# Half of each w_in piece on a second DMA queue, and a new written order for every engine, in an attention block followed by a feed-forward layer

## The chip, the cores and the metric

The kernel runs on one core of one Trainium2 chip. The metric is the device time of one execution in microseconds (us), lower is better. Three runs of the kernel before took 711.14, 709.20 and 710.52 us; the median is 710.52.

## What is computed

Inputs are x (8 batches, 8 heads, 512 tokens, 64 wide), state (8, 8, 32, 64), w_in (512 x 2048) and w_out (2048 x 512), all float32.

```python
scores = x @ state.T / sqrt(D);  a  = softmax(scores);   xread = a  @ state
scores2 = state @ x.T / sqrt(D); a2 = softmax(scores2);  sread = a2 @ x
t = concat([xread, sread], axis=2)      # 544 rows a head; heads side by side: 4352 x 512
h = t @ w_in
out = (h * erf(softplus(h))) @ w_out
```

## The kernel before, in words

The batches are worked off one after another. Batch 0 goes its own way at the start (`begin0`, `mixed0`, `first0`, `serf0`, `second0`); the others use seven products in place of eight for each pair of block matrices, in the first product (`first_product`, L930) and in the second (`second_product`, L1014, and a twice nested form, `twice_product`, L1250). `mixed` and `mixed0` multiply the states of a batch by w_in; the attention weights (tile aT) times that (tile m) give h.

d_ff is cut into 16 columns of 128. A **piece** of w_in is one such column: 512 x 128, laid in SBUF as 128 partitions of 4 runs of 128 floats. `rows_in` (L524) loads a piece in two DMAs, partitions 0 to 63 (e = 0) and 64 to 127 (e = 1). Pieces 0 to 7 are fetched at the start, in four pairs, by `fetch_in` through SyncE's queue; pieces 8 to 15 ("late") through GpSimd's queue between batches, next to the late pieces of w_out (`fetch_out`). The early part of w_out comes in four pairs of 1 MB on SyncE's queue (L564).

A piece lands in one of three staging tiles, raw 0 to 2, and is converted (`convert`): two ScalarE passes (L547 writes the piece, L549 works on raw in place), then three VectorE passes (L551, L553, L555). After the last of these its raw tile is free for the next fetch. The early pairs go in this order with their tiles: w_in 0-1 (raw 0), w_in 2-3 (raw 1), w_out 0-1 (raw 2), w_out 2-3 (raw 0), w_in 4-5 (raw 1), w_in 6-7 (raw 2), w_out 4-5 (raw 0), w_out 6-7 (raw 1).

The start of batch 0: x arrives in four DMAs, TensorE transposes it (L404), the copies x0 to x3 bring it to SBUF, scores (L430), copies s00 to s11, transposes of the scores (L436), softmax on VectorE and ScalarE (L455, L457, L460, L462, L465), transposes of a (L440), the copies ta0 and ta1 into aT, and the first products of batch 0 (L602) with the m tiles of `mixed0` (L585). softplus (L609), erf (L614) and a multiplication (L618) follow, then the second products (L627). `warm` (L114) issues filler products.

What sets the order: every step is recorded by `op` with an engine, a cost and the regions that it reads and writes. ORDER (L163) is a table written out by hand: for each engine, the sequence in which its recorded steps are issued. `emit` lays the steps of all engines into one program by a small simulation with the costs, and `in_order` ties each engine to its sequence. An engine issues strictly in that order, so a step that waits holds all steps behind it on its engine, DMA issues included. `either` puts a copy out of PSUM on VectorE if its name is in BY_VECTOR (L153), else on ScalarE.

Of the kernel before, what the change touches and what calls it, by code (L numbers as in the profile page):

```python
# [17 lines left out]
def kernel(  # L18
# [17 lines left out]
    nc = tc.nc  # L36
# [6 lines left out]
    NK = d_model // P  # L43
# [55 lines left out]
    begun = traced()  # L99
# [39 lines left out]
    def op(engine, cost, at, go, reads=(), writes=(), table=None, land=0.0, pipe=0.0):  # L139
# [14 lines left out]
        x0 x1 x2 s10 ta1 m021 u1""".split())  # L154

    def either(name, cost, out, in_, at, reads, writes):
# [3 lines left out]
        else:  # L160
# [4 lines left out]
            8 0-1 5 2 15 3 6 4 9 7 12 16 13 10 17 11 14 18-21 23 22 25 24 37 45 61 36 60 53 44 52 62  # L165
            26 46 55 27 38 29 28 47 30-32 49 48 41 39 68 34 51 33 50 35 43 66-67 40 65 42 69 63 84
            54 70 58-59 72-73 64 74 71 75 77 76 80 57 85 81 78 86 56 79 87 83 82 89 88 93-94 90 122
            121 97-98 124 123 91 125 128 95-96 127 99 126 101 92 102-103 131 104 129-130 132 100 109
            105-106 110 133 107-108 134-135 111 113 112 114 136 138 115-116 168 140-142 169-171
            117-119 175 144 143 120 145 172 146 137 173 148-149 147 177-178 150 174 179 156 152-153  # L170
            151 157 176 180 154 139 181 155 182-183 160 185 158 161-163 215-216 159 218 217 187-189
            219 190 164-167 195 220 196 221-222 184 191 225 224 223 199 226 192 200 227 201-202 197
            186 228 193-194 198 229-230 207 232 208-210 203 262 204-205 265 206 264 266 263 211 234
            212 267 235 213-214 236 269 231 238 237 239-240 272 250 268 241-242 271 273 246 243 247
            233 248 270 244 249 275 274 245 251-252 254 276 255 253 256-257 277 281 279 282 278 309
            283 285 310 312 286 284 313 311 258 287 259-260 316 261 293 314-315 289 318-319 288 294
            280 320 290-291 321 317 292 295 322 296-297 323-324 301 355 302 298 303-304 356 299-300
            325 358 305-306 359 307 357 326 308 327 361 360 334 329 362 336 328 335 365 337 364 338
            331 363 366 330 332 367 340 339 368 348 333 397 341 398 342 399 401 343 350 349 344 352
            402 351 345 353 346-347 354 369 400 376 370 378 377 379-380 371 381-382 372-373 390 374  # L180
            403-404 375 405 383 406 384-387 407-410 391 425 392 426 393-394 431 388 432 389 429-430
            427 395 428 433-434 396 415 435-437 439 416 411 438 413 412 440 417 414 419 456 455 420
            418 458 423 457 459 421-422 462 460 424 461 465 443 445 464 466 463 446 467-468 441-442
            444 447 449 470 450 469 448 451 453 499 454 452 502 500-501 471 503 506 478 504 472-473
            479 474 480 505 482 509 481 475 483 508 476 510 477 507 511 485 512 484 486 492 488 514
            487 513 493-494 489 543 490 496 495 545 497 546 544 491 547 498 550 548 522 515 524 549
            526 517 516 519 553 523 552 554 525 551 555 527 518 520 528 556 536 557-558 521 537-538
            529 539-540 587 531 530 533 532 542 590 541 566 589 588 535 568 594 591 567 534 570
            592-593 569 559 597 560-561 598 595 563 596 562 599 572 564 600 571 565 602 601 580 573
            632 631 575 582 581 574 577 634 633 576 583-584 635 578 585-586 636 638 610 579 637  # L190
            640-641 612 603 642 611 613-614 639 615 643 604 616 605-606 644 607 645 608 646 609 624
            617 625-626 619 627 675 618 621 620 678 628 622 677 630 629 654 679 655 657 623 656 676
            682 647 658 680-681 648-650 659 685 684 660 651 686 683 668 687 652 688 653 689 661 690
            670 662-664 669 671 719-720 672 665 673 721 674 722 666 726 667 723 691 698 724 700 725
            693 692 694 729 702 699 701 730 703 727 695 728 732 731 696 704 733 712 734 714 697 713
            705 763 715-716 707 706 766 764 709 708 717 765 710 718 711 742 767 743 745 744 735
            768-769 737 736 746 738 770 747 739 773 772 748 774 771 740 775-776 756 741 757 749
            758-759 751 750 752-753 760 754-755 761-762 777 784 778-780 786 781 785 788 787 789 783
            790 782 791 798 793 792 795 794 800 796-797 799 802 805 801 807 806 803 809 808 804
            810-811""",  # L200
        ACT: """
            0-1 3 10-11 5 4 2 13 12 6-7 16-17 30 9 31 15 33 14 8 32 19 59 18 58 34 36 35 38 40 20-21
            39 37 41 22-24 43 42 25-27 44 46-47 45 48-50 53 52 51 61 29 60 64 56 54 67 55 62 57 68
            63 70 97 69 28 98 109 71 108 73 101 72 74 66 105 75 80 102 99 82 100 76-77 83 103 79 78
            89 104 84 81 90 139-140 137-138 85 141 88 86 142 87 152 65 93 154 153 94 155 106-107
            95-96 91 148 92 156 110 161 143 149 163 144-146 164 162 157 111 158 160 112 165 168 113
            150 166-167 175 174 159 147 114 169-170 177-178 176 171 117 115 179 189 151 190 116 119
            118 172-173 191 185 180 192 182 193 198 181 120 183 200 195 199 123 201 203 194 124 186
            121 202 122 204 184 205 187 211-212 197 214 213 196 125 215 206-207 216 226 208 188 209
            227-228 130 127 129 126 210 128 229 222 219 230 235-237 135 217 238 220 218 232-233 239  # L210
            134 224 240 231 131 221 133 136 223 241 248-249 132 243 234 250-251 242 252-253 263 244
            265 225 245 266 246 256 264 247 257 254 267 272 255 274 259 273 275 271 278 269 258 277
            268 261 270 276 280 279 281 285-286 260 282 262 288 287 289 283 290 300 284 302 301 291
            296 303 292 304 309 311 310 293-294 312 314 313 295 315 307 297 316 308 305 298 323 322
            306 325 324 317-321 347 299 349-350 326 348 327 351 332 356 334 333 328 358 357 355 335
            353 330 359 329 352 354 331 360 362 336 363 361 364-365 337 366 342 389 367 343 368 338
            345 344 339-340 346 341 390 369 374-375 377 376 370-372 391 373 379 378 392 380 393 384
            396 395 382 394 397 381 385 402 398-399 386-387 404 400-401 403 383 405-406 409 388 416
            410 417-418 415 408 407 420 411-413 422 421 414 423 425 424 429 426 431 428 432 430 435
            433 436 434 427 437-441 419 442-445 466 468 467 446 469 451 472 470 452 475 448 454 447  # L220
            453 477 449 476 478 474 480 471 450 455 479 456 473 481-485 491 461 457 488 486 458
            489-490 459 462 487 512 464 513 460 514 465 463 515 497-498 492-493 516 521 500 523 518
            495 524 499 494 527 522 525 528 501 496 507 519 526 517 534 520 529-530 508 502 536 531
            535 537 510 503 509 532-533 558 505 560 504 559 511 543 561 544 506 562 567 538 546 569
            564 539 570 541 545 571 568 566 540 574 573 542 563 565 583 582 580 575 547 572 548 553
            576-577 581 549 604 578 606 551 554 556 550 607 555 605 557 579 552 589 608 613 615 610
            590 614 591 616 592 584 612 585 619 586 617 587 621 611 626 593 588 620 628 618 609 599
            629 594 622-623 595 600-601 624 627 650 625 597 602 652 596 603 635 653 598 651 636-637
            630 638 656 654 659 661 631 657 633 662 639 655 645 658 663 632 665 660 666 664 634 672
            667 640 668-669 674-675 646 670 673 641 671 648 647 696 642-643 697-698 644 699 676 649  # L230
            681-682 700 705 707 684 677 708 703 683 704 679 678 706 702 701 709 711 685 712 718 713
            691 680 720 719 710 721 714 686 692 715-716 742 717 694 687 689 693 688 695 744 727 690
            743 745 722 748 728 730 750 723 746 724 751 729 725 753 749 731 747 752 754 726 756-757
            755 758 737 759-760 732 761-762 733 763 738 734-735 740 736 739 764 741 769 765 770
            766-767 772 771 773 768 774 779 775 777 776 780 778 784 781-783""",
# [1469 lines left out]
```

## Time and profile before

| | |
|---|---|
| median of three runs | 710.52 us |
| the profiled execution | 708.29 us |
| its span, first to last instruction | 706.5 us |
| TensorE busy | 693.0 us (98%) |
| VectorE busy | 592.3 us (84%) |
| ScalarE busy | 469.6 us (66%) |
| GpSimd busy | 89.8 us (13%) |
| mean granted TensorE clock | 0.997 |
| SyncE's and ScalarE's DMA queues | 61.88 and 0.52 MB |
| GpSimd's DMA queue | 29.63 MB |

How to read it: PE is TensorE, PEld its weight loads, DVE VectorE, ACT ScalarE, POOL GpSimd, SP SyncE; a q behind a name is the engine's sequencer, which issues DMAs. L627 is line 627 of the kernel. A row of the timeline has the start, the duration, the engine, the line, the operation, out<-in, shapes and count, and in brackets the idle time before it with what ended it. A row of the windows has a stretch, its length, busy time and count of instructions for PE, PEld, DVE, ACT and POOL, the granted clock (1.00 is full), the busy share of the 16 DMA engines and GB/s. The line "DMA to landing" gives the least, median and largest time from issue to landing. One float32 product is two MATMUL records.

### The profile page before, as it was taken

Reading aid. Unit: us, or ns where it says so; the run is one execution under the profiler, and the core shown is the slowest. Engines: PE = TensorE matmul, PEld = TensorE weight load, DVE = VectorE, ACT = ScalarE, POOL = GpSimd, SP = SyncE. Lnnn points to the kernel's source line nnn. Section 1 sums busy time; section 2 is a strip of 40 time slices with the busy share of each in tenths; the row PEclk is TensorE's granted clock in tenths of the full one; section 3 lists DMA queues with packets and bytes.
Section 4 is the critical chain, followed back from the end, with each engine's and each line's share of the span. In section 5 each row is a group of like instructions: output and inputs, shape, how many; then the busy total and the mean of one; then the engine's idle time right before and its main releaser. Section 6 shows DMA issues by size and latency. Waiting matters only on the chain.

```text
span 706.5 us, 13126 instructions
## 1 busy us (share of the span) xinstructions
PE 693.0 (98%) x5163; PEld 579.7 (82%) x5163; DVE 592.3 (84%) x986; ACT 469.6 (66%) x852; POOL 89.8 (13%) x101
## 2 busy tenths in 40 slices
PE   8899999999999999999999999999999999999997
PEld 7334568787878878799999879898989898989996
DVE  5889999999999989797945489696869695877897
ACT  5887798878688474837254674838585757575741
POOL 0001101103010100000100100121023214052222
PEclk9999999999999999999999999999999999999999
DMA  9876998777796926221365410325156535285645
GB/s 238 196 192 120 257 235 208 191 179 210 177 291 140 313 97 187 91 83 31 109 169 221 116 53 30 83 32 97 16 97 75 98 45 98 46 105 61 100 65 104
DMA packets 132620, 92.85 MB, mean 131 GB/s; under 512 B 92624, under 2 KB 119632, under 8 KB 132048
## 3 DMA queue, kind: packets, MB, share of 16 engines
q1 hardware_dynamic: 113088, 61.88, 32.7%
q0 software_dynamic: 18928, 29.63, 23.6%
q8 instruction: 40, 0.66, 0.4%
q10 hardware_dynamic: 544, 0.52, 0.2%
q14 instruction: 20, 0.16, 0.1%
HBM read 50.86 MB, written 41.16 MB: 130 GB/s over the span
## 4 chain that ended last, share of the span: by engine, by line
PE 84%; DVE 6%; DMA 2%; ACT 2%; issue 1%; DVEq 0%; SPq 0%
PE o L1250 28%; PE h L930 18%; PE o L1014 17%; PE at L930 7%; PE o L1433 4%; PE h L1384 3%; DMA raw<-in_moe_w_out_dram 2%; PE h L831 2%; PE at L831 2%; PE at L794 1%; PE at L1384 1%; PE h L689 1%; DVE w_in L1232 1%; DVE ring L981 1%; DVE ring L970 1%
## 5 line engine op out<-in xcount | busy, mean ns | idle before, releaser
L942 ACT COPY ring<-h 128x512 f32<-128x512 f32 x120 | 69.1, 587 | 72.9 <-PE h L930 67.5
L930 PE MATMUL h<-aT,m 128*128 128x256 f32 x360 | 91.4, 381 | 0.2 <-ACT ring L942 0.2
L970 DVE TENSOR_TENSOR ring<-ring 128x1024 f32<-128x1024 f32 (+1 forms) x64 | 72.9, 1151 | 22.3 <-ACT ring L967 22.3
L1014 PE MATMUL o<-w_out,ring 128*128 128x256 f32 x320 | 78.0, 382 | 0.0
L952 ACT ACTIVATE ring<-ring 128x512 f32<-128x512 f32 x120 | 72.6, 635 | 3.9 <-DVE ring L944 3.3
L930 PEld LDWEIGHTS h<-aT,m 128*128 128x128 f32 x360 | 65.3, 190 | 10.5 <-ACT ring L942 1.3
L981 DVE TENSOR_TENSOR ring<-ring 128x1024 f32<-128x1024 f32 x60 | 72.5, 1217 | 0.3
L1014 PEld LDWEIGHTS o<-w_out,ring 128*128 128x128 f32 x320 | 59.7, 190 | 15.6 <-issue 5.2
L1250 PE MATMUL o<-w_out,w_in 128*128 128x128 f32 x512 | 69.6, 276 | 0.0
L1250 PEld LDWEIGHTS o<-w_out,w_in 128*128 128x128 f32 x512 | 64.7, 192 | 3.6 <-issue 0.8
L1250 PE MATMUL o<-w_out,ring 128*128 128x128 f32 x480 | 64.8, 276 | 0.0
L1250 PEld LDWEIGHTS o<-w_out,ring 128*128 128x128 f32 x480 | 60.4, 192 | 3.7 <-DVE ot L1265 0.8
L967 ACT ACTIVATE ring<-ring 128x1024 f32<-128x1024 f32 (+1 forms) x64 | 62.7, 1004 | 0.2
L1014 PE MATMUL o<-raw,ring 128*128 128x256 f32 x240 | 59.2, 381 | 0.0
L1014 PEld LDWEIGHTS o<-raw,ring 128*128 128x128 f32 x240 | 45.2, 190 | 7.9 <-issue 1.7
L1250 PE MATMUL o<-raw,ring 128*128 128x128 f32 x360 | 49.7, 275 | 0.0
L1250 PEld LDWEIGHTS o<-raw,ring 128*128 128x128 f32 x360 | 46.0, 192 | 1.9 <-DVE oo L1265 0.8
L1170 POOL DMA_DIRECT2D out_dram<-oo x16 | 23.4, 1462 | 174.6 <-ACT o L1281 104.0
L1250 PE MATMUL o<-raw,xT 128*128 128x128 f32 x320 | 41.1, 276 | 0.2 <-DVE m L1265 0.2
L1250 PEld LDWEIGHTS o<-raw,xT 128*128 128x128 f32 x320 | 38.7, 192 | 1.6 <-issue 0.8
L1281 ACT COPY o<-o 128x256 f32<-128x256 f32 (+1 forms) x41 | 13.5, 330 | 26.8 <-PE o L1250 17.8
L930 PE MATMUL h<-sy,m 128*128 128x256 f32 x120 | 31.1, 382 | 0.0
(269 smaller groups left out, 1421.5 us busy)
## 6 DMA issues: line engine op xcount, KB each, us to landing
x<-in_x_dram SPq DMA_DIRECT2D x30, 256.0 KB, 4.6
xq<-in_x_dram SPq DMA_DIRECT2D x24, 256.0 KB, 4.8
out_dram<-oo SPq DMA_DIRECT2D x10, 512.0 KB, 3.7
raw<-in_moe_w_in_dram SPq DMA_DIRECT2D x16, 256.0 KB, 5.2
raw<-in_moe_w_out_dram SPq DMA_DIRECT2D x4, 1024.0 KB, 7.9
raw<-in_moe_w_in_dram POOLq DMA_DIRECT2D x16, 256.0 KB, 5.3
raw<-in_moe_w_out_dram POOLq DMA_DIRECT2D x8, 512.0 KB, 4.3
kept_a<-aT SPq DMA_DIRECT2D x8, 512.0 KB, 4.7
```

Source lines behind the costliest of these rows:

```text
L831: nc.tensor.matmul(out=bank(names[e])[q, :], lhsT=st[r, b, q], rhs=of_group[2 * u + j][r, :, i, :], start=True, stop=True)
L930: nc.tensor.matmul(out=out_[:, i], lhsT=x_[:, q:q + P], rhs=y_, start=(start and i == 0), stop=(i == 1), skip_group_check=not start)
L942: op(ACT, 0.5, t, lambda: nc.scalar.copy(out_(), view(bank(name))), [name], w)
L952: op(ACT, 0.53, t, lambda: nc.scalar.activation(out=part(splane, k), in_=part(hplane, k), func=ACTF.Softplus), area(hplane, ks=[k], os=[o] ...
L967: op(ACT, 0.085 + 0.875 * share, at + n, lambda s_=s_: nc.scalar.activation(out=s_, in_=s_, func=ACTF.Erf), [], area(splane, ks=[k], os=os ...
L970: op(DVE, 0.065 + 1.075 * share, at + n + 1, lambda s_=s_, h_=h_: tt(s_, s_, h_, op=ALU.mult), area(hplane, ks=[k], os=os), area(splane, k ...
L981: op(DVE, 1.14, at + k, lambda k=k, x_=x_, y_=y_, how=how: tt(get("h", k), get(*x_), get(*y_), op=how), area(v[x_[0]], ks=[x_[1]]) + area( ...
L1014: nc.tensor.matmul(out=view(name)[:, h], lhsT=lhs[:, i, :], rhs=weight_of[n]()[:, u, i, :], start=(start and h == 0 and i == 0), stop=(h = ...
L1170: op(GP, 1.2, t, lambda: nc.gpsimd.dma_start(out=quad(r, c), in_=one(v), accum_op=ALU.add), every(*v), [("out", b, r, c)], land=3.0, pipe=2.0)
L1250: nc.tensor.matmul(out=out_[:, Q2 * k:Q2 * k + Q2], lhsT=lhs[:, k, i], rhs=rhs[:, i], start=first, stop=(k == len(ns) - 1 and i == 1), ski ...
L1384: nc.tensor.matmul(out=bank(bk)[:, P * i:P * i + P], lhsT=x_[:, i, k], rhs=y_[:, k], start=(start and i == 0 and k == 0), stop=(i == GF - ...
L1433: nc.tensor.matmul(out=bank("o%d" % bk)[:, E2 * c:E2 * c + E2], lhsT=ring[:, w_[w], plane, k][:, i, :], rhs=weight_of[n]()[:, u, i, :], st ...
```

## The change

`rows_in` takes two queues, one for each half of the partitions. The first half of an early piece stays on SyncE's queue. The second half goes through ScalarE's queue for pieces 0 and 1 and through GpSimd's for pieces 2 to 7. Late pieces have both halves on GpSimd's queue, as before.

```diff
-    def rows_in(on, to, f, n):
-        for e in range(2):
+    def rows_in(queues, to, f, n):
+        for e, on in enumerate(queues):
             on.dma_start(out=to[D * e:D * e + D],
                          in_=moe_w_in[NI * D * e:NI * D * (e + 1), P * f:P * (f + n)].rearrange(
                              "(k d) f -> d k f", d=D).bitcast(U32))

     def fetch_in(f, k, h, at, late=False):
-        how, on = late_load if late else ((SP, 0.9), nc.sync)
-        op(*how, at, lambda: rows_in(on, half(k, h).rearrange("p (a b) -> p a b", a=NK), f, 1),
-           [("out0", 1)] * late, RAW(k, [h]), land=3.0 * late, pipe=1.7)
-
-    late_load = (GP, 2.0), nc.gpsimd
+        queues = (nc.gpsimd if late else nc.sync, nc.scalar if f < 2 else nc.gpsimd)
+        op(GP if late else SP, 2.0 if late else 0.5, at, lambda: rows_in(
+            queues, half(k, h).rearrange("p (a b) -> p a b", a=NK), f, 1),
+           [("out0", 1)] * late, RAW(k, [h]), land=(3.0 if f > 1 else 0.0),
+           pipe=2.5 if late else 1.7)
```

Which copies VectorE makes is chosen anew, and ORDER is a new table for all five engines (not shown in full: it is a list of step numbers). The simulation in `emit` now always takes the engine whose next step can begin first, where it ran each engine as far as it could.

```diff
     BY_VECTOR = set("""
-        x0 x1 x2 s10 ta1 m021 u1""".split())
+        x0 x1 s01 ta0 m010 m011 m020 u0 u1""".split())
```

What the new order does to the built program, in the lines of the kernel before:

- TensorE: 2611 matrix instructions before and after. The start has 8 + 5 + 3 + 14 filler products where it had 2 + 8 + 3 + 17. Of the first L602 products the second pair now comes first, with transposes of the states and one `mixed0` among the others.
- VectorE after the last L465: m copy, aT copy (ta0), m copy, then the conversions; before: a scale, w_out, w_in (both conversions), then the aT copy (ta1).
- ScalarE: two DMA issues at the head (the second halves of pieces 0 and 1). The m copies of `mixed0(1, 0)` stand ahead of the conversion of w_out 4-5 instead of behind it, and the conversion of w_out 6-7 behind softplus and erf of the next two first products instead of ahead of them. 838 instructions instead of 840: two table loads fewer.
- SyncE: the second half of batch 1's xq loads (four DMAs of 128 KB, L93) stands ahead of the load of w_out 6-7 instead of behind it.
- GpSimd: six half pieces at the head of its queue.
- From batch 1 on, the steps of all engines are in another sequence; the last 158 matrix instructions stand together at the end in both.

More of the change, by code (lines that the diff above doesn't have):

```diff
@@ L170 @@
[L170 to L184, printed above, removed]
@@ new lines @@
+            0-2 5 3 6 8 15 9 13 4 7 16 12 10 17 11 14 20 23 18 21 19 22 25 24 44 36-37 60 53 52 61
+            45 26 38 27 29 28 47 30-32 46 63 48 64 49 39 56 50 34 51 54 43 33 41-42 68 55 40 35 70
+            69 84 59 66-67 73 72 74 71 62 65 75 77 76 80 58 78 81 85 57 79 82 86 83 93 88 87 94
+            89-90 97 121 98 122 124 123 125 95 128 126 96 99 127 101 91 131 102 129 103 132 130 92
+            100 133 105-106 134 107 104 135 109-110 108 136 113-115 111 116 138 112 168 140-142 170
+            143 117 171 118 148 119 169 175 149 172 120 137 173 144 174 145 177 156 178 150 157 179
@@ new lines @@
+            176 152 180 146 181-182 151 147 158 139 153 159 183 154-155 185 160-161 216 187 162-163
+            215 188-190 217 164 218 165 184 219 191 166 192 220 222 167 193 195 221 199 225 196 224
+            186 226 223 200 227 201 194 229 228 197 202 198 230 232 207-209 203 262 210 204 265
+            205-206 263 266 231 264 211-212 234-235 213 236-237 269 267 242-243 214 271 244 268
+            246-248 272 233 238-240 249-250 273 270 245 274 241 275-276 254-255 277 251-252 279 253
+            256-257 309 281-283 310 258 311 284 259-260 312 316 289 278 261 290 313 285 291 314 286
@@ L301, in emit @@
         while any(queue.values()):
-            before = len(end)
+            ready = []
             for e, line in queue.items():
-                while line and all(m in end for m in ops[line[0]][4]):
-                    n = line.popleft()
-                    _, cost, _, _, needs, table, land, pipe = ops[n]
-                    begin[n] = max([free[e]] + [end[m] + LAG[ops[m][0]] * (
-                        ops[m][0] != e or ops[m][7] > 0) for m in needs])
-                    if table not in (None, loaded):
-                        cost, loaded = cost + 1.28, table
-                    end[n] = free[e] = begin[n] + cost
-                    if pipe:
-                        piped = max(piped, begin[n]) + pipe
-                        end[n] = max(piped, free[e]) + (land or FIXED)
-                        if e == SP:
-                            free[e] = max(free[e], piped - AHEAD)
-            assert len(end) > before
+                if line and all(m in end for m in ops[line[0]][4]):
+                    n = line[0]
+                    ready.append((max([free[e]] + [end[m] + LAG[ops[m][0]] * (
+                        ops[m][0] != e or ops[m][7] > 0) for m in ops[n][4]]), n, e))
+            begun, n, e = min(ready)
+            queue[e].popleft()
+            begin[n] = begun
+            _, cost, _, _, _, table, land, pipe = ops[n]
+            if table not in (None, loaded):
+                cost, loaded = cost + 1.28, table
+            end[n] = free[e] = begun + cost
+            if pipe:
+                piped = max(piped, begun) + pipe
+                end[n] = max(piped, free[e]) + (land or FIXED)
+                if e == SP:
+                    free[e] = max(free[e], piped - AHEAD)
         order = sorted(begin, key=lambda n: (begin[n], n))
```

205 lines of the change are left out of this document (105 added, 100 removed), and 6 rows, old and new, of the table ORDER.

## The prediction

> **What bounds the kernel now.** First the page's heading, then busy time by stage, then the stretches with gaps.
>
> ```profile
> span 706.5 us, 13126 instructions
> ```
> ```profile
> 70.00:200.00 130.00, 129.77 (x936) 99.47 (x935) 128.37 (x226) 105.48 (x185) 18.64 (x32) 1.00 0.86 212
> 200.00:660.00 460.00, 459.74 (x3452) 407.50 (x3451) 367.70 (x603) 292.03 (x549) 57.73 (x51) 1.00 0.45 103
> ```
> Columns: length, busy PE, PEld, DVE, ACT, POOL, granted clock, DMA share, GB/s. From 70 to 660 us TensorE lacks 0.23 + 0.26 = 0.5 us. The change touches no product, and both builds issue 2611 matmuls, so nothing is to be won there. VectorE misses only 1.6 us of the 130 up to 200, so there is something to lose.
>
> ```profile
> 5.00:10.00 5.00, 5.00 (x67) 4.15 (x66) 2.36 (x4) 1.90 (x4) 0.00 (x0) 1.00 1.12 239
> 10.00:15.00 5.00, 3.20 (x64) 2.19 (x63) 4.74 (x10) 3.40 (x8) 0.00 (x0) 1.00 1.08 307
> 15.00:20.00 5.00, 4.35 (x50) 3.74 (x49) 4.86 (x11) 2.64 (x5) 0.00 (x0) 1.00 1.08 258
> 20.00:25.00 5.00, 2.13 (x6) 1.25 (x7) 3.80 (x8) 4.50 (x8) 0.00 (x0) 0.82 1.04 227
> ...
> 40.00:45.00 5.00, 4.20 (x24) 1.16 (x22) 3.89 (x6) 3.75 (x5) 0.00 (x0) 1.00 1.07 362
> 45.00:50.00 5.00, 4.80 (x26) 1.96 (x27) 3.98 (x6) 3.77 (x5) 0.00 (x0) 1.00 0.48 77
> 50.00:55.00 5.00, 4.53 (x12) 1.77 (x10) 4.63 (x6) 4.94 (x8) 0.00 (x0) 1.00 0.00 0
> 55.00:60.00 5.00, 4.83 (x24) 1.66 (x23) 4.97 (x7) 4.73 (x7) 0.00 (x0) 1.00 0.36 59
> ```
> ```profile
> 700.00:706.50 6.50, 1.98 (x18) 1.79 (x17) 2.34 (x9) 0.00 (x0) 0.00 (x0) 0.95 0.39 124
> ```
> Before 25 us the DMA engines are full and VectorE is nearly so, while TensorE partly runs filler products. From 40 to 60 its pauses sum to 0.80 + 0.20 + 0.47 + 0.17 = 1.6 us. The last 4.5 us are the drain, which ends in the same 158 products in both builds. So the end is set by when the first large product (L602) starts, plus a fixed queue of products, plus pauses. That start, in order of time:
>
> ```profile
> 20.36 0.69 DVE L465 TENSOR_TENSOR ring<-ring,z1b 128x512 f32<-128x512 f32 x1
> 20.50 1.17 ACT L549 ACTIVATE raw<-raw 128x1024 uint32<-128x1024 uint32 x1 [2.86 <-DMA raw<-in_moe_w_in_dram]
> ...
> 21.11 0.66 PE L440 MATMUL o<-ident,ring 128*128 128x128 f32 x4 [1.76 <-DVE ring L465]
> ...
> 21.71 1.11 ACT L547 ACTIVATE w_in<-raw 128x1024 f32<-128x1024 f32 x1
> 22.73 0.58 ACT L161 COPY aT<-o 128x512 f32<-128x512 f32 x1
> ...
> 23.19 0.28 ACT L161 COPY m<-h 128x128 f32<-128x128 f32 x1
> ...
> 23.47 0.68 DVE L159 COPY aT<-o 128x512 f32<-128x512 f32 x1
> 23.52 5.21 PE L602 MATMUL h<-aT,m 128*128 128x512 f32 x8 [1.76 <-ACT m L161]
> ```
> ScalarE stands 2.86 us before the conversion of w_in pieces 2 and 3, whose DMA lands at 20.5; the copies of aT and m that L602 needs are queued behind it and end at 23.5.
>
> **The change part by part.** *Issues.*
>
> ```profile
> 0.00:5.00 5.00, 3.64 (x17) 3.64 (x18) 0.00 (x0) 1.28 (x1) 0.69 (x6) 1.00 0.63 177
> ```
> ```profile
> 1.74 1.41 SPq L526 DMA_DIRECT2D raw<-in_moe_w_in_dram  x2
> ...
> 3.83 1.41 SPq L526 DMA_DIRECT2D raw<-in_moe_w_in_dram  x2
> 5.29 0.60 SPq L564 DMA_DIRECT2D raw<-in_moe_w_out_dram  x1
> 6.11 2.85 SPq L526 DMA_DIRECT2D raw<-in_moe_w_in_dram  x4
> ```
> A half piece costs SyncE about 0.7 us. Four of the first eight leave it (2.8 us), so its last early issue ends near 9.0 - 2.8 = 6.2. ScalarE takes two (1.4 us), in a stretch where it has one instruction of 1.28 us to do. GpSimd, idle then, issues the second halves of pieces 2 and 3 from about 1.4 us on. Earlier issue is not earlier landing: the DMA share is above 1 from 5 us, so the same bytes fill the engines until about 20. What can be won is the beginning: a share of 0.63 in the first 5 us leaves 1.8 us free. I take 1.0: pieces 2 and 3 at 19.5 (bounds 20.5 and 18.7).
>
> The Trainium skill (DMA: Bandwidth & Descriptors, section Rules for kernel authors) says not to split a transfer into partition halves on two queues, since both use the same 16 DMA engines and only issue time is saved. The shares above 1 agree; by that rule alone pieces 2 and 3 stay at 20.5, which is the first rival.
>
> *The order at the start.* Of VectorE's work up to the last multiplication (L465):
>
> ```profile
> L159 DVE COPY xT<-o 128x512 f32<-128x512 f32 x1 | 0.7, 692 | 0.6 <-PE o L404 0.6
> ...
> L159 DVE COPY ring<-o 128x256 f32<-128x256 f32 x1 | 0.4, 411 | 0.0
> ```
> ```profile
> 21.57 0.16 DVE L477 TENSOR_SCALAR m2b<-m2b 128x2 f32<-128x2 f32 x1
> ```
> The 0.69 us copy x2 goes to ScalarE; a 0.16 scale (L477) moves ahead; one 0.41 copy replaces another. The chain shortens by 0.5, of which I take 0.2, because the second score copies, now both on ScalarE, arrive late. L465 then ends at 20.85 instead of 21.05. Behind it VectorE now does one m copy, the first aT copy and the second m copy, ahead of the weight work. An m copy on VectorE is not in the trace; it lies between 0.16 (128x2) and 0.41 (128x256), and I take ScalarE's 0.28 for this shape. So 20.85 + 0.28 + 0.68 = 21.8: the first half of the first L602 starts there instead of 23.52, **-1.7 us**. Its second half needs ScalarE's aT copy, still behind pieces 2 and 3: 19.5 + 1.17 + 1.11 + 0.58 = 22.4. The first half is two of the 8 records that took 5.21 us, 1.3 us, and runs until 23.1, so nothing is lost. If they land at 20.5 it is 23.4, a pause of 0.3.
>
> *The clock.*
> ```profile
> 23.00:26.00 3.00, 2.48 (x3) 1.17 (x4) 2.97 (x4) 3.00 (x6) 0.00 (x0) 0.53 0.85 133
> ```
> TensorE stood idle for 1.76 us before the transpose of 21.11 and for 1.76 more after it; then the clock is granted at 0.53 for these 3 us, 1.4 us lost. A shorter thin stretch may avoid it. Bounds 0 and -1.4; I take 0, since the stretch before 21.8 still waits for the same L465 and holds only that 0.66 us transpose. The Trainium skill (TensorE: Matmul & The Clock Gate, section Part 1) puts the window that drops the clock near 3.4 us; the dip is of that length, and by that rule the shorter stretch stands just at the edge.
>
> *From 26 to 65.* Two of the pauses:
>
> ```profile
> 45.20 1.98 PE L602 MATMUL h<-aT,m 128*128 128x512 f32 x4 [0.79 <-ACT m L161]
> ...
> 51.87 3.70 PE L602 MATMUL at<-aT,m 128*128 128x512 f32 x8 [0.47 <-ACT m L161]
> ```
> The first is an m copy behind a wait for w_out's third pair; the new order puts that copy ahead of the conversion, so 0.8 goes. Late next is w_in pieces 6 and 7, which two copies now stand behind: I give back 0.4. Against this stands SyncE's order:
>
> ```profile
> 39.38 0.39 SPq L564 DMA_DIRECT2D raw<-in_moe_w_out_dram  x1
> 39.82 7.69 SPq L93 DMA_DIRECT2D xq<-in_x_dram  x4
> ```
> ```profile
> 47.43 1.17 ACT L547 ACTIVATE w_out<-raw 128x1024 f32<-128x1024 f32 x1 [1.21 <-DMA raw<-in_moe_w_out_dram]
> ...
> 53.91 1.06 ACT L614 ACTIVATE ring<-ring 128x1024 f32<-128x1024 f32 x1
> ```
> The four xq loads (7.69 us of issue) now come before the last w_out pair. Issued from about 35, they hold that pair until 42.5 instead of 39.4, so it lands near 50.5 instead of 47.4. The new order has ScalarE first finish softplus and erf (L614) of the second group's first two products. That erf ended at 55.0; without the 1.21 of waiting and two conversions of 1.17 ahead of it, and 1.7 earlier, it ends at 49.8. This cover is 0.7 us short. ScalarE then waits 0.7 where it waited 1.21, and TensorE has second products (L627) left over, so I charge 0.1, with bounds 0 and +3.1 (no cover at all). GpSimd's halves of pieces 4 to 7 replace SyncE's; both landings are in the trace:
>
> ```profile
> L526 POOL DMA_DIRECT2D raw<-in_moe_w_in_dram x4: 630/640/672, 66.6 to 74.0; - x4
> ...
> DMA to landing us min/median/max: 5.6/6.8/7.0
> ```
> ```profile
> L526 SPq DMA_DIRECT2D raw<-in_moe_w_in_dram x8: 595/615/1467, 26.6 to 35.0; - x8
> ...
> DMA to landing us min/median/max: 3.8/4.5/5.1
> ```
> GpSimd's median is 2.3 us slower than that of SyncE's eight halves of these pieces; two SyncE issues fewer per pair save about 1.4. Net 0 to +0.9 a pair, hidden behind softplus and erf. I take +0.1.
>
> *The rest.* Two table loads fewer on ScalarE, off the path. The order of 70 to 660 us is new throughout: 0 taken, bounds below.
>
> Sum: -1.7 - 0.8 + 0.4 + 0.1 + 0.1 = **-1.9 us**. The profiled execution took 708.29 (span 706.5, 1.8 around it), hence 706.4; the median of the runs shown is 710.52, hence **708.6**.
>
> **The rivals.** *The split brings nothing:* pieces 2 and 3 land at 20.5, the pause of 0.3 comes, and ScalarE's conversions, 1.0 later, hold the next steps by what the pause has not taken: -1.9 + 0.3 + 0.7 = -0.9, 709.6. For: shares above 1. Against: 1.8 us of free engines before 5.
> *Clock and pauses too:* -1.9 - 1.4, and half of the 0.8 us of pauses left: -3.7, 706.8. For: the 0.53 row. Against: the thin stretch shrinks by only 1 us.
> *The xq loads take the lead:* they cost their bound, -1.9 - 0.1 + 3.1 = +1.1, 711.6. For: no cover shows in the trace for a pair that lands at 50.5. Against: the second products (L627) can be put in between.
> *Slower, VectorE is late in 70 to 200:* it is busy 128.37 of 130 there and feeds every product. ScalarE meets conversions of late pieces in order, as here:
>
> ```profile
> 79.59 0.71 ACT L549 ACTIVATE raw<-raw 128x512 uint32<-128x512 uint32 x1 [2.26 <-DMA raw<-in_moe_w_out_dram]
> ```
> One such wait was hidden. There are 16 late pieces; once the waits exceed VectorE's 1.6 us of slack, each further one goes to the end. Three waits of 2.26 less 1.6 are 5.2, less the 1.9 won: +3.3, 713.8. For: all orders are new, and 0.5 us of pauses can hardly be bettered. Against: the same lead of 1.7 us reaches these loads.
>
> **How the numbers follow.** About 0.3% (2.1 us) is what a measurement of this kernel can tell from no change. Chances: forecast 0.45 (706.8 to 709.8 by the bounds of its terms, with 0.24 of it beyond 2.1 us), clock and pauses 0.14, no gain from the split 0.09, the xq loads 0.08, slower 0.24. Faster is 0.24 + 0.14 = 0.38; within 0.3% is 0.21 + 0.09 + 0.08 = 0.38; slower 0.24. The range 705.5 to 713.8 leaves out half of the slow case and a tail of the fast one.
>
> **What would show it.** Right: L602's first product near 21.8, pieces 2 and 3 converted from 19.5, no 0.79 pause at 45, TensorE without pauses from 70 to 660. Wrong: L602 later than 23, ScalarE waiting over 2 us for the last w_out pair near 50, or VectorE idle for more than 4 us between 70 and 200.

## The result, and the profile after

The changed kernel took 707.52 us (median of 20 runs, 706.02 to 709.03) against 709.20 us of the kernel before (20 runs, 705.53 to 711.76): ratio 0.9975, 95% interval 0.9964 to 0.9986, so 1.8 us (1.0 to 2.6) less. The forecast was 708.6 from 710.52, a gain of 1.9. The size is right. The profiles show that it was reached by another way. One execution of run 8 below (795.44 us, at a granted clock of 0.851) is left out of its comparison.

The profiled execution took 709.03 us (span 707.0), the slowest of the 20, and 0.7 above the profiled one of before. So the pair is read for where time moved, and sums are made with two profiles of each kernel, of which the second is in the experiments. Windows of the changed kernel, columns as before:

```profile
5.00:10.00 5.00, 5.00 (x65) 4.13 (x66) 2.46 (x4) 1.33 (x3) 0.00 (x0) 1.00 1.05 223
10.00:15.00 5.00, 2.97 (x48) 2.22 (x49) 2.69 (x6) 2.53 (x5) 0.00 (x0) 0.86 1.10 292
15.00:20.00 5.00, 4.78 (x47) 4.05 (x31) 4.36 (x9) 3.16 (x8) 0.00 (x0) 0.50 1.15 249
20.00:25.00 5.00, 4.27 (x43) 3.19 (x41) 4.21 (x12) 3.48 (x7) 0.00 (x0) 0.96 0.82 238
40.00:45.00 5.00, 4.49 (x25) 1.52 (x24) 3.67 (x5) 3.89 (x6) 0.00 (x0) 1.00 0.92 246
45.00:50.00 5.00, 4.72 (x26) 1.73 (x25) 4.70 (x7) 4.00 (x5) 0.00 (x0) 1.00 0.84 208
50.00:55.00 5.00, 4.83 (x15) 1.67 (x17) 4.56 (x7) 4.97 (x8) 0.00 (x0) 1.00 0.14 57
55.00:60.00 5.00, 5.00 (x24) 2.11 (x24) 5.00 (x8) 4.95 (x7) 0.00 (x0) 1.00 0.62 100
70.00:200.00 130.00, 129.74 (x993) 98.81 (x992) 128.00 (x224) 104.77 (x182) 11.69 (x21) 1.00 0.85 208
200.00:660.00 460.00, 460.00 (x3448) 408.44 (x3447) 369.33 (x606) 290.39 (x546) 61.00 (x59) 1.00 0.45 101
```

From 10 to 15 us VectorE has 2.69 us of work where it had 4.74: it waits for data. From 15 to 20 the clock is granted at 0.50; before, the low clock lay at 23 to 26. From 40 to 60 TensorE's pauses are 0.51 + 0.28 + 0.17 + 0.00 = 1.0 us instead of 1.6. From 70 to 660 they are 0.3 instead of 0.5, and VectorE has 2.0 us of slack up to 200.

The start, in rows of the timeline (lines beyond 305 are 4 higher than before: L602 is now L606, L404 is L408, L547 is L551):

```profile
11.63 0.66 ACT L551 ACTIVATE w_in<-raw 128x512 f32<-128x512 f32 x1 [2.48 <-DMA raw<-in_moe_w_in_dram]
...
12.85 0.66 PE L408 MATMUL o<-ident,x 128*128 128x128 f32 x4 [1.81 <-DMA x<-in_x_dram]
...
18.90 1.14 ACT L551 ACTIVATE w_out<-raw 128x1024 f32<-128x1024 f32 x1 [1.68 <-DMA raw<-in_moe_w_out_dram]
...
24.42 1.13 PE L606 MATMUL h<-aT,m 128*128 128x512 f32 x2 [0.34 <-DVE m L159]
```

and the first three of these steps in the kernel before:

```profile
8.44 0.67 ACT L547 ACTIVATE w_in<-raw 128x512 f32<-128x512 f32 x1 [0.88 <-DMA raw<-in_moe_w_in_dram]
...
9.55 0.66 PE L404 MATMUL o<-ident,x 128*128 128x128 f32 x4
...
14.52 1.17 ACT L547 ACTIVATE w_out<-raw 128x1024 f32<-128x1024 f32 x1 [0.88 <-DMA raw<-in_moe_w_out_dram]
```

The first w_in piece is converted at 11.63, where it was 8.44; the last x part is transposed at 12.85, where it was 9.55; the first w_out pair is converted at 18.90, where it was 14.52. The first large product starts at 24.42: not 1.7 earlier than 23.52 but 0.9 later. The DMA view of the first 26 us has, for each issue, its count, its size and the median time to landing, of the changed kernel:

```profile
raw<-in_moe_w_in_dram SPq DMA_DIRECT2D x4, 256.0 KB, 11.8
...
raw<-in_moe_w_in_dram POOLq DMA_DIRECT2D x2, 256.0 KB, 7.5
raw<-in_moe_w_in_dram ACTq DMA_DIRECT2D x2, 256.0 KB, 10.3
```

and of the kernel before:

```profile
raw<-in_moe_w_in_dram SPq DMA_DIRECT2D x8, 256.0 KB, 8.2
```

GpSimd's halves of pieces 2 and 3, which nobody needs before about 20 us, are issued at 1.5 and 2.3 and take 6.2 and 8.8 us. The halves of pieces 0 and 1, which are needed at once, take 9.0 and 9.5 on SyncE's queue and 9.7 and 10.9 on ScalarE's, where all four took 5.4 to 7.0 before. (The 11.8 is a median over SyncE's halves of all four pieces.)

### The profile page after: what moved, and what is told of

Same layout as the page of the kernel before. It is cut to its first block, busy times and chain, and to the rows that moved or that the text cites. A ratio compares the mean times of both kernels' runs of the same rounds, so it can differ in the third digit from the quotient of the medians.

```text
span 707.0 us, 13147 instructions
## 1 busy us (share of the span) xinstructions
PE 695.6 (98%) x5163; PEld 582.5 (82%) x5163; DVE 593.2 (84%) x988; ACT 467.6 (66%) x848; POOL 94.8 (13%) x107
## 4 chain that ended last, share of the span: by engine, by line
PE 88%; DVE 4%; DMA 4%; ACT 3%; issue 1%; SPq 0%; POOL 0%; DVEq 0%; ACTq 0%
PE o L1254 28%; PE h L934 18%; PE o L1018 17%; PE at L934 7%; PE o L1437 4%; PE o L631 3%; PE h L1388 3%; PE h L835 2%; PE at L835 2%; DMA x<-in_x_dram 1%; DMA raw<-in_moe_w_out_dram 1%; PE at L798 1%; PE at L1388 1%; PE h L693 1%; DMA raw<-in_moe_w_in_dram 1%; DVE w_in L1236 1%
## 5 line engine op out<-in xcount | busy, mean ns | idle before, releaser
L1018 PEld LDWEIGHTS o<-raw,ring 128*128 128x128 f32 x240 | 44.7, 190 | 11.8 <-issue 5.0
L948 DVE TENSOR_TENSOR ring<-ring,at 128x512 f32<-128x512 f32 x30 | 20.5, 683 | 14.7 <-ACT ring L946 9.2
L934 PE MATMUL h<-sy,sx 128*128 128x256 f32 x120 | 31.1, 382 | 0.3
```

Source lines behind the costliest of these rows:

```text
L934: nc.tensor.matmul(out=out_[:, i], lhsT=x_[:, q:q + P], rhs=y_, start=(start and i == 0), stop=(i == 1), skip_group_check=not start)
L1018: nc.tensor.matmul(out=view(name)[:, h], lhsT=lhs[:, i, :], rhs=weight_of[n]()[:, u, i, :], start=(start and h == 0 and i == 0), stop=(h = ...
```

## The experiments

The twelve kernels ran in three groups of four (1 to 4, 5 to 8, 9 to 12), each group beside runs of the kernel before on the same chip. Theory A is the prediction: the split brings the pieces earlier and the start forward. Theory B: the halves on other queues make the data needed first come later, and the new order wins that back. B1, B2, C and D are told where they come in. The table has the median and the ratio first, then times (us) in the one profiled execution: first w_in conversion, transposes of the last x part, first large product (L602), first second product (L627), and where the granted clock lay below 1.

| kernel | median | ratio to before, interval | w_in | x | L602 | L627 | low clock |
|---|---|---|---|---|---|---|---|
| before, as predicted from | 709.20 | | 8.4 | 9.6 | 23.5 | 33.5 | 23-27 |
| changed, result | 707.52 | 0.9975 [0.9964, 0.9986] | 11.6 | 12.9 | 24.4 | 35.1 | 13-21 |
| 1 changed again | 707.13 | 0.9970 [0.9960, 0.9980] | 11.3 | 12.4 | 24.3 | 34.3 | 23-28 |
| 2 split alone | 710.16 | 1.0014 [1.0004, 1.0024] | 11.4 | 12.4 | 26.0 | 35.3 | 11-22 |
| 3 order alone | 705.14 | 0.9953 [0.9936, 0.9971] | 8.7 | 10.3 | 21.4 | 32.1 | none |
| 4 before again | 708.77 | 1.0000 [0.9987, 1.0013] | 8.5 | 9.6 | 23.8 | 35.3 | 23-30 |
| 5 ScalarE's halves only | 705.42 | 0.9946 [0.9932, 0.9961] | 8.7 | 10.2 | 21.2 | 33.9 | 22-29 |
| 6 GpSimd's halves only | 707.75 | 0.9989 [0.9978, 1.0000] | 10.9 | 11.8 | 23.5 | 33.4 | none |
| 7 GpSimd's of 4 to 7 only | 705.71 | 0.9949 [0.9935, 0.9964] | 9.3 | 10.9 | 22.2 | 31.7 | none |
| 8 changed, more filler | 706.43 | 0.9968 [0.9957, 0.9980] | 11.3 | 12.2 | 23.6 | 34.1 | none |
| 9 changed, GpSimd held | 704.59 | 0.9940 [0.9928, 0.9952] | 8.6 | 10.4 | 21.2 | 32.1 | none |
| 10 as 5, more filler | 705.16 | 0.9942 [0.9929, 0.9955] | 8.9 | 10.3 | 22.7 | 33.8 | 14-18 |
| 11 as 3, more filler | 704.64 | 0.9940 [0.9928, 0.9952] | 9.7 | 11.0 | 22.8 | 33.4 | none |
| 12 order alone again | 707.00 | 0.9965 [0.9951, 0.9978] | 8.4 | 10.0 | 21.1 | 33.5 | 22-29 |

### 1 to 4: the two halves of the change apart

Run 1 is the changed kernel, run 4 the kernel before, unchanged. Run 2 is the kernel before with the split of the queues only; run 3 is the changed kernel without it:

```diff
-        queues = (nc.gpsimd if late else nc.sync, nc.scalar if f < 2 else nc.gpsimd)
+        queues = (nc.gpsimd, nc.gpsimd) if late else (nc.sync, nc.sync)
```

> The changed kernel as it is, for a second trace. Theory A (as predicted: the first large product starts near 21.8 us and the lead of 1.7 us is kept): the start at 24.42 us in the first trace was an untypical execution, and here the product starts before 23.5. Theory B (the halves on three queues let the pieces land later: 11.6 us instead of 8.4 for the first piece and 12.8 for the last part of x; the new order wins the time back after 25 us): it starts after 24 again, w_in's first conversion not before 11. Both: 1.2 to 2.4 us faster than the kernel before.

> The kernel before with its old orders, the second halves of the early pieces on ScalarE's and GpSimd's queue. Theory A: pieces 2 and 3 land 1 us earlier, the 2.86 us wait before their conversion shrinks, 0.5 to 1.2 us faster than before. Theory B: the first piece and the last part of x land 1 to 3 us later, the start of the first large product moves by the same, and it is 1 to 3 us slower.

> The changed kernel with both halves of each early piece on SyncE's queue, as before; orders, copies and all else are those of the changed kernel. Theory A: pieces 2 and 3 land 1 us later than with the split, 0.5 to 1.2 us slower than the changed kernel, so 0.6 to 1.3 faster than before. Theory B: the first conversion starts near 8.5 to 9 again, the first large product near 22, and it is 1 to 3 us faster than the changed kernel, so 3 to 5 faster than before.

> The kernel before as it is, for a second trace and as a measure of the noise. Both theories: 0.999 to 1.001 of the kernel before, first large product at 23.5, the 2.86 us wait at 20.5 within 0.5 us. If the first trace was untypical, these two move.

The split alone is 1.0 us slower (0.3 to 1.7), the order alone 3.3 us faster (2.1 to 4.5; in run 12 again 2.5, 1.6 to 3.5), where both together gain 1.8 (the result) to 2.1 (run 1). Theory A falls. (That the order alone beats the changed kernel doesn't follow from these runs by themselves, as the intervals of runs 3 and 12 overlap with those of the result and run 1; runs 5 and 9 below bear it out.) In the split alone (its lines are 1 higher than before beyond L526):

```profile
11.35 0.66 ACT L548 ACTIVATE w_in<-raw 128x512 f32<-128x512 f32 x1 [4.69 <-DMA raw<-in_moe_w_in_dram]
```
```profile
12.37 1.11 PE L404 MATMUL o<-ident,x 128*128 128x128 f32 x4 [3.66 <-DMA x<-in_x_dram]
```

Both stand 3 us later than in the kernel before, after waits of 4.69 and 3.66 us. In the order alone they are nearly where they were (0.2 and 0.8 us later):

```profile
8.68 0.68 ACT L551 ACTIVATE w_in<-raw 128x512 f32<-128x512 f32 x1
```
```profile
10.31 0.60 PE L408 MATMUL o<-ident,x 128*128 128x128 f32 x4
...
21.39 1.13 PE L606 MATMUL h<-aT,m 128*128 128x512 f32 x2 [0.34 <-DVE m L159]
```

The start that the prediction put at 21.8 comes at 21.39, but in the kernel without the split.

### 5 to 7: which queue, which pieces

Each is the changed kernel with another line for the queues of early pieces (late ones have both halves on GpSimd's queue in all): in run 5 only pieces 0 and 1 are split (the first new line), in run 6 only 2 to 7 (the second), in run 7 only 4 to 7 (the third).

```diff
-        queues = (nc.gpsimd if late else nc.sync, nc.scalar if f < 2 else nc.gpsimd)
+        queues = (nc.gpsimd, nc.gpsimd) if late else (nc.sync, nc.scalar if f < 2 else nc.sync)
+        queues = (nc.gpsimd if late else nc.sync, nc.sync if f < 2 else nc.gpsimd)
+        queues = (nc.gpsimd if late else nc.sync, nc.sync if f < 4 else nc.gpsimd)
```

> The changed kernel with only pieces 0 and 1 split (second halves on ScalarE's queue); pieces 2 to 7 wholly on SyncE's queue. Theory B holds that the split makes the data needed first come later; it leaves open by which queue. B1 (GpSimd's halves of pieces 2 and 3, issued at 1.5 us ahead of everything but the first x parts, take the bandwidth): without them the first w_in conversion starts near 8.7 us, the first large product near 21.4, the time is that of the order alone, 3.3 us below before (705 to 706). B2 (ScalarE's halves of pieces 0 and 1 are what lands late): conversion stays at 11.3 to 11.6, first product near 24.3, time 1.5 to 2 us below before, as the changed kernel.

> The changed kernel with pieces 0 and 1 wholly on SyncE's queue and the second halves of pieces 2 to 7 on GpSimd's. B1: the halves of pieces 2 and 3 still move ahead of pieces 0 and 1, so the first conversion is late by 1 us or more (9.7 to 11.6 instead of 8.7) and the time 1 to 2 us above the order alone, about as the changed kernel. B2: conversion near 8.7, first large product near 21.4, 3.3 us below before. Theory A, as predicted (pieces 2 and 3 come earlier and bring the start forward): first large product before 21.4 and more than 3.3 us below before.

> The changed kernel with pieces 0 to 3 wholly on SyncE's queue and only the second halves of pieces 4 to 7 on GpSimd's, issued when their staging tiles come free. The prediction's fourth term gives these halves +0.1 us, up to +0.9 a pair. B1: same start as the order alone (conversion 8.7, first large product 21.4), time within 0.5 us of it, 2.8 to 3.3 us below before. If GpSimd's queue itself were costly at any place: 1 us or more above the order alone, with a wait of VectorE or ScalarE for a w_in piece after 25 us.

B1 holds: runs 5 and 7 keep the gain of the order (3.8 and 3.6 us by the ratios), run 6 loses most of it (0.8). Run 6, with the halves of pieces 2 and 3 on GpSimd's queue:

```profile
10.87 0.66 ACT L551 ACTIVATE w_in<-raw 128x512 f32<-128x512 f32 x1 [2.49 <-DMA raw<-in_moe_w_in_dram]
```
```profile
23.52 1.12 PE L606 MATMUL h<-aT,m 128*128 128x512 f32 x2 [0.34 <-DVE m L159]
```

and run 5, with ScalarE's halves of 0 and 1 but no GpSimd ones:

```profile
8.74 0.69 ACT L551 ACTIVATE w_in<-raw 128x512 f32<-128x512 f32 x1 [0.44 <-DMA raw<-in_moe_w_in_dram]
```
```profile
21.16 1.39 PE L606 MATMUL h<-aT,m 128*128 128x512 f32 x2 [0.34 <-DVE m L159]
```

The conversion is 10.87 - 8.68 = 2.2 us later in run 6 than in the order alone, and the first large product 23.52 - 21.39 = 2.1. Two halves of 256 KB are 0.52 MB; at the 239 GB/s that the kernel before moves from 5 to 10 us they are 2.2 us of transfer. So the price at the start is about the plain time of the bytes that went ahead.

One profile does not measure this closely, as the start scatters. In the seven profiles of the new order without GpSimd's early halves (runs 3, 5, 7, 9 to 12) the first large product starts at 21.1 to 22.8 us; run 7, expected at 21.4, is at 22.2. In the four with them (the result, runs 1, 6, 8) it starts at 23.5 to 24.4. The ranges don't meet, and their means, 21.8 and 24.0, are 2.2 apart. At the first second product 1.3 of this is left (32.9 and 34.2).

### 9: the same halves, later

Run 9 is the changed kernel with one instruction more: GpSimd copies one word of the last x part to a spare tile, so that its DMAs behind it start later (piece 3 is issued ahead of piece 2).

```diff
+        if f == 3:
+            nc.gpsimd.tensor_copy(kept_tile("hold", lambda: small.tile([1, 1], F32, name="holdb", bufs=1)),
+                                  kept_tile("x", None)[0:1, 3, 0, 0:1])
         for e, on in enumerate(queues):
```

> The changed kernel, with one more GpSimd instruction: a copy of one word of the last x part into a spare tile, ahead of GpSimd's first half pieces (of pieces 2 and 3). The same halves go through the same three queues, but GpSimd's first two start only when the last x part is in, near 10 us, not at 1.5. B1, in the narrow form (what costs is that these 0.25 MB move ahead of piece 0 and the last x part): first w_in conversion near 8.8 us, last x part near 10.2, first large product 21.2 to 22.2, and 3 to 3.8 us below before, like the split of pieces 0 and 1 alone. If what costs is that GpSimd's queue carries halves of these pieces at all: conversion or pieces 2 and 3 late all the same, first large product after 23, at most 2 us below before.

(The two halves are 0.52 MB by the page, not the 0.25 of this text: `convert` reads every weight as a pair of 32-bit words, so w_in and w_out arrive with 64 bits a number, not as the float32 named under "What is computed".) GpSimd's part of the timeline, then ScalarE's and TensorE's (lines 3 higher than in the changed kernel):

```profile
10.12 0.17 POOL L530 COPY holdb<-x 1x1 f32<-1x1 f32 x1 [8.81 <-DMA x<-in_x_dram]
10.23 1.43 POOL L533 DMA_DIRECT2D raw<-in_moe_w_in_dram  x2
```
```profile
8.57 0.68 ACT L554 ACTIVATE w_in<-raw 128x512 f32<-128x512 f32 x1
```
```profile
21.23 1.13 PE L609 MATMUL h<-aT,m 128*128 128x512 f32 x2 [0.34 <-DVE m L159]
```

The same bytes go through the same queues, only at 10.2 instead of 1.5, and the conversion is back at 8.57, the first large product at 21.23, the median 4.3 us below before, somewhat more than the 3 to 3.8 expected. It is not the queue that costs but the place in time. This version keeps the change and beats both kernels: its whole interval (0.9928 to 0.9952) lies below that of the changed kernel (0.9964 to 0.9986). So do those of runs 5, 10 and 11; between these four the runs don't tell a best one.

### 8, 10, 11 and 12: the clock

Theory C: TensorE's waits before the first large products bring its clock down, and filling them keeps it. Rival D: the fall costs nothing, or the filler holds up the start. Run 8 is the changed kernel, 10 is run 5 and 11 is run 3, each with more filler (10 and 11: 20 products in place of 14, nothing else); 12 repeats run 3.

```diff
-            spare_products("o%d" % g, 3 if g else 14, 12.6 + 5 * g)
+            spare_products("o%d" % g, 3 if g else 22, 12.6 + 5 * g)
...
-    spare_products("h0", 3, 10.7)
+    spare_products("h0", 8, 10.7)
```

> The changed kernel with 5 more filler products behind those at 9.1 us and 8 more behind those at 16.4 us; nothing else is touched, the result is the same. In the changed kernel's two profiles the granted clock falls to 0.50 once, from 13.8 to 20.4 us in the one and from 23.9 to 27.9 in the other, each time 2.0 to 2.8 us after TensorE began a wait of 1.4 to 2.6 us; the order alone had waits of 1.9 at most and no fall. Theory C (these waits bring the clock down): with the waits filled the clock stays at 1.00 up to 30 us, the first eight large products are not stretched, and the time is 1 to 1.7 us below the changed kernel's (705.5 to 706.5, with before near 709). Rival D (the fall does not follow from these waits, or the filler itself holds up the start): clock still 0.50 somewhere before 30 us or first large product after 24.8, time within 0.5 us of the changed kernel's or above.

> The new order with only pieces 0 and 1 split (second halves on ScalarE's queue), and 6 more filler products behind those at 14 us. In the profile without them the clock fell to 0.50 from 22 to 28.7 us and the stretch from the first large product to the first second product took 12.8 us instead of 10.7. Theory C: no fall below 1.00 before 30 us, that stretch 9.6 to 10.7 us, and a median below 705 (0.3 to 1.5 us under the same without filler, 3.4 to 3.8 below before). Rival D (a fall lies beside waits for data and costs nothing in the median, as with the filler in the changed kernel): 3.2 to 4 us below before, not to be told from the same without filler.

> The new order with every early piece wholly on SyncE's queue, and 6 more filler products behind those at 14 us. Theory C: executions in which the clock falls no longer do so; the median is 0.3 to 1 us below the order alone of the same call. Rival D: the same as the order alone within 0.3 us; the profile shows the same start, first large product near 21.4.

> The new order alone once more, as the base of this call: 3.0 to 3.8 us below before; if the profile of it catches a fall of the clock, the stretch from the first large product to the first second product grows from 10.7 to some 12 us.

The windows from 20 to 30 us of the order alone (run 3):

```profile
20.00:25.00 5.00, 2.91 (x8) 1.01 (x8) 4.44 (x8) 4.29 (x6) 0.00 (x0) 1.00 1.00 270
25.00:30.00 5.00, 4.93 (x31) 2.39 (x32) 4.86 (x7) 4.95 (x7) 0.00 (x0) 1.00 0.93 196
```

and of the same kernel in run 12:

```profile
20.00:25.00 5.00, 3.90 (x8) 1.27 (x9) 4.34 (x8) 4.30 (x6) 0.00 (x0) 0.68 0.95 252
25.00:30.00 5.00, 5.00 (x29) 2.16 (x29) 3.27 (x6) 3.74 (x6) 0.00 (x0) 0.64 0.97 193
```

One program, nearly the same waits (1.90 and 1.87 us before the second transposes of a), and the clock falls in one execution and not in the other: the stretch from the first large product to the first second product is 10.7 us in run 3 and 12.4 in run 12. Six profiles have a wait of 1.87 to 1.95 us at this place: runs 5 and 12 have the fall and take 12.8 and 12.4 us for the stretch, runs 3, 6, 7 and 9 have none and take 9.6 to 10.9. Run 1 doesn't fit: it has the fall after a wait of 2.58 us, and its stretch is 10.0; why is open. The Trainium skill (TensorE: Matmul & The Clock Gate, section Part 1) says that the clock follows a window of activity that runs freely and is not tied to the start of a kernel; executions of one program with and without the fall agree with that, while no run here shows the window itself.

With the filler in the changed kernel (run 8) the clock stays up:

```profile
15.00:20.00 5.00, 4.75 (x41) 4.57 (x42) 4.71 (x10) 2.86 (x8) 0.00 (x0) 1.00 1.15 249
20.00:25.00 5.00, 3.78 (x36) 2.16 (x34) 4.49 (x11) 3.97 (x7) 0.00 (x0) 1.00 0.73 200
```

and in the eleven executions that count the granted clock is 0.995 to 1.000, with 0.999 in the middle, against 0.993 to 0.998 over the 20 of the result. So C holds for the fall. For the price it does not: 1 to 1.7 us below the changed kernel was expected, and by the ratios to the kernel before on the same chip run 8 is 0.5 us below the result (0.9968 against 0.9975) and 0.1 below run 1 (0.9970), which is what rival D expected of the time.

Run 11 is 1.8 us below run 12 of its own group by the ratios (0.9940 against 0.9965, the intervals meeting at 0.9951 to 0.9952) and 0.9 below run 3 (0.9953), so "0.3 to 1" is neither shown nor refuted. Run 12 itself gained 2.5 us where 3.0 to 3.8 was expected.

Run 10 failed its expectation. Its profile has a fall at 14 to 18 us, just as the filler begins, and the slowed filler then holds up the start, the second case of D. It runs from 14.66 to about 20.7, the transposes of a behind it no longer wait for VectorE, and the first large product comes at 22.7, where run 5 has 21.2:

```profile
14.66 6.13 PE L114 MATMUL o<-ident 128*128 128x128 f32 x40
...
21.10 1.09 PE L444 MATMUL o<-ident,ring 128*128 128x128 f32 x8
```

This execution was not typical: the granted clock is 0.999 or more in the five others, against one of six in run 5, so the filler keeps the clock here too. Still the median is not to be told from that of run 5 (0.9942 against 0.9946).

That a fall goes with a longer execution is also seen within the result: the 9 executions of the changed kernel with a granted clock of 0.996 or more have a median of 706.56, the 11 below that 708.18, 1.6 us more. But what the filler wins by keeping the clock lies between 0.1 and 1.8 us by the ratios, so the price of a fall in the median stays open.

## Why the prediction was right, step by step

**The first step failed: the start, -1.7 us.** The prediction let pieces 2 and 3 land 1.0 us earlier, out of the 1.8 us in which the DMA engines are free in the first 5, and moved nothing else. Nothing of that free time was used. The first 5 us of the changed kernel have a DMA share of 0.61 and 179 GB/s, where they had 0.63 and 177:

```profile
0.00:5.00 5.00, 3.88 (x17) 3.65 (x18) 0.00 (x0) 1.28 (x1) 2.13 (x8) 1.00 0.61 179
```

Instead, the bytes at the head of an idle queue went ahead of pieces 0 and 1, the last x part and the first w_out pair. Measured: the first large product came later by 0.9 and 0.5 us (24.42 and 24.28 against 23.52 and 23.77), and so later than 23, which the prediction itself had named as a sign of being wrong. In the changed kernel's second profile (run 1) the way is this:

```profile
19.61 1.16 ACT L551 ACTIVATE w_out<-raw 128x1024 f32<-128x1024 f32 x1 [2.97 <-DMA raw<-in_moe_w_out_dram]
20.67 0.61 ACT L464 ACTIVATE ring<-ring 128x512 f32<-128x512 f32 x1
```
```profile
23.28 0.67 PE L444 MATMUL o<-ident,ring 128*128 128x128 f32 x4 [2.58 <-DVE ring L469]
```

The exponential of the second softmax half (L464) is queued behind the conversion of a w_out pair that waits 2.97 us for its DMA; the transposes of a follow 2.58 us late. For the order the reasoning from VectorE's shorter chain fits: without GpSimd's early halves the start is 21.1 to 22.8, in the mean of seven profiles the 21.8 that was forecast. Nor did the pieces themselves come sooner: a piece is there when its later half is, and in the changed kernel the last half of pieces 2 and 3, which SyncE issued at 6.8, took the longest of all halves in the first 26 us, 14.9 us:

```profile
DMA to landing us min/median/max: 6.2/9.6/14.9
```

That is near 21.7, not 19.5, and later than the 20.5 of the kernel before.

The rule of the Trainium skill (DMA: Bandwidth & Descriptors, section Rules for kernel authors), which the prediction quoted, that halves on two queues share the same engines and only issue time is saved, is borne out as far as it goes. The rival built on it, "the split brings nothing" (709.6), was nearer in its reason than the forecast, but too kind: the split alone cost 1.0 us.

**The pauses: -0.8 + 0.4 expected, about -2.3 measured.** From the first second product to the end of the span the kernel before needs 706.5 - 33.5 = 673.0 and 709.0 - 35.3 = 673.7 us, the changed one 671.9 and 670.2: 2.3 less on average, where the prediction's terms for this part sum to -0.8 + 0.4 + 0.1 + 0.1 = -0.2. Windows from the first second product to 60 us, of the kernel before:

```profile
33.54:60.00 26.46, 24.83 (x97) 9.32 (x97) 23.82 (x31) 23.61 (x30) 0.00 (x0) 1.00 0.59 150
```

and of the changed kernel in run 1 and in the result:

```profile
34.31:60.00 25.69, 25.68 (x100) 10.51 (x100) 24.60 (x35) 24.17 (x29) 0.30 (x1) 1.00 0.79 181
```
```profile
35.14:60.00 24.86, 23.90 (x94) 9.26 (x94) 22.61 (x32) 22.65 (x28) 0.00 (x0) 1.00 0.71 168
```

TensorE lacks 1.63 us before, 0.01 and 0.96 after. With 60 to 660 us added the sums are 2.1 (2.9 in run 4) before and 0.2 and 1.2 after, 1.8 less on average; the last 0.5 of the 2.3 is not assigned. The gain goes with the new order, split or not. From the first second product to the end the eleven profiles with it (the result, runs 1, 3 and 5 to 12) need 669.9 to 671.9 us, the three with the old order 673.0, 673.7 and, with the split (run 2), 672.6.

The pause of 0.79 at 45.20 went, as the step said, but so did the 0.47 at 51.87 and the smaller ones, which the prediction listed and didn't count. The -0.8 was also read from one execution: run 4, the same kernel, has no pause near 45 and one of 1.26 us at 53.57. The 0.4 given back for pieces 6 and 7 fits as a mean of two: the result has their waits, 0.51 + 0.28, and run 1 has none. In the result ScalarE stands before their conversion, with the m copies behind it:

```profile
42.31 1.16 ACT L551 ACTIVATE w_in<-raw 128x1024 f32<-128x1024 f32 x1 [1.10 <-DMA raw<-in_moe_w_in_dram]
...
44.40 0.63 ACT L161 COPY m<-at 128x256 f32<-128x256 f32 x2
...
44.81 1.98 PE L606 MATMUL h<-aT,m 128*128 128x512 f32 x4 [0.51 <-ACT m L161]
...
47.08 0.67 PE L589 MATMUL at<-w_in,ring 64*32 64x256 f32 x16 [0.28 <-DVE w_in L559]
```

**The two terms of 0.1.** The last w_out pair is converted without a wait, here and in run 1:

```profile
52.48 1.06 ACT L618 ACTIVATE ring<-ring 128x1024 f32<-128x1024 f32 x1
53.44 1.13 ACT L551 ACTIVATE w_out<-raw 128x1024 f32<-128x1024 f32 x1
```

so the xq loads cost nothing and their rival (711.6) is out. GpSimd's halves of pieces 4 to 7 cost nothing that can be told (run 7 at 0.9949, run 3 at 0.9953).

**The clock: 0 taken.** The mean held, the reading did not: the fall was taken as part of the stretch before 21.8, and it is a matter of chance from one execution to the next, at 13 to 21 us or at 23 to 28 in the changed kernel. The stretch from the first large product to the first second one took 10.0 and 11.5 us before, 10.7 and 10.0 after.

**70 to 660 us: 0 taken,** and right: TensorE's pauses there are 0.3 instead of 0.5, and the slow rival (three waits for late pieces, 713.8) did not come.

Together: +0.7 for the start, -0.4 up to the first second product, -2.3 from there, -2.0 us, against the measured 1.8. That the total was forecast right was luck: the start, over-rated by 2.4, and the part from the first second product on, under-rated by 2.1, cancelled.

## What to carry to other kernels

Here a second queue added no bandwidth (177 GB/s in the first 5 us before, 179 after), but it took away order: what was issued on an idle queue at the start went ahead of what waited its turn on the busy one. Before moving a transfer, ask for each load when it is due, and what lands later by the time of the bytes put ahead; hold a load that is due late behind a dependency on one that is due first. And a forecast whose total fits should still be checked term by term: here two errors of over 2 us hid each other.

## What was not expected of the hardware

SyncE's second w_in issue waited where the queues were split: the waits of its queue in run 1 name 1.6 us for an x part to land ahead of an L530, and in the timeline of the changed kernel the issue that stood at 3.83 before comes at 4.75:

```profile
2.54 0.59 SPq L393 DMA_DIRECT2D x<-in_x_dram  x1
4.75 0.63 SPq L530 DMA_DIRECT2D raw<-in_moe_w_in_dram  x1
```

The gap goes with ScalarE's halves: runs 5 and 9, which have them, have it too (4.79 and 4.70) and lose nothing by it, while run 6, which has only GpSimd's, issues at 3.87 and on without it. It also put the end of SyncE's early issues at 7.4 us, where the prediction had 6.2. Why the issue waits was not tried.

The granted clock goes with much of the scatter of the changed kernel, whose every execution does the same work: 1.6 us between the two groups of the 20 executions, nearly as much as the whole gain of the change. It does not account for all of it: in run 6 one execution took 709.83 us at a clock of 0.998 and another 708.22 at 0.993.
